# An attention block and two expert layers on one Trainium2 core: the second expert layer keeps its whole first expert unscaled, and three pieces of its order of work are rearranged

## The chip, the cores and the metric

The kernel runs on one core of a Trainium2 chip. The metric is the device time of one execution in microseconds (us), and of several executions the median. The kernel must return the reference's output, 3072 x 512 float32 numbers, to the accuracy asked for.

## What is computed

An attention over chunks, a first expert layer with one expert per token, and a second expert layer that runs all eight experts on every token. The change touches only the second layer. Cut to it, the reference is

```python
x = moe(attention(q, k, v, mem_k, mem_v))      # (N, D) = (3072, 512)
logits = x @ w_gate                            # (N, E), E = 8
P = np.exp(logits - logits.max())
for _ in range(8):                             # sinkhorn
    P /= P.sum(1, keepdims=True) + 1e-09
    P /= P.sum(0, keepdims=True) + 1e-09
    P *= N / E
out = np.zeros((N, D))
for e in range(E):
    h = np.maximum(x @ w1[e], 0.0)             # w1[e] is (512, 1024)
    out += P[:, e:e + 1] * (h @ w2[e])         # w2[e] is (1024, 512)
```

The plan P (a factor for each token and expert) needs eight rounds over all tokens before the first output can be scaled.

## The kernel before, in words

**Units.** Tokens are worked on in six blocks of 512 (NS = 6). An expert takes 12 units (EU), two for each block, one for each half of the hidden features; eight experts make 96 units, n = 0 to 95, and the loop over n runs to 96 so that the last outputs get done. Both products are done by a Strassen-like scheme of seven products (numbers 0 to 6) in place of eight, of 12 matmuls each, on operands that are split into a high and a low part, three matmuls for each piece of work. So a unit has 84 hidden matmuls (`h_mm`, L949 to L951), and among them stand the output matmuls of the unit before (`y_mm`, L1018 to L1020). The list TURN sets the order: "h0", "h1", "h5" and so on are hidden products, "y" is the next output product, "end" the end of the unit. Blocks end in units whose n is even ("even units"): there the last two output products (`y_tail`) come in as well, and the finished block is scaled and put out in the unit behind (an "odd unit").

**Hidden products.** `h_done` empties PSUM behind each product: for h0 ScalarE (ACT) copies the bank to the one that h1 adds to (L964), for the others ACT applies the relu (L916) or VectorE adds (L850). From the results, seven operands `cb0` to `cb6` for the output products are made: a cast to the high part on ACT (`c_hi`, L925 or L916) and a difference for the low part on VectorE (`c_lo`, L915 or L917). Those of cb5 and cb2 are in `h_rest`, at the unit's end.

**Outputs.** `y_done` and `y_end` gather a finished block in two tiles, oA and oB, one buffer each: ACT scales by P (`scaled`, L1035), VectorE adds with the factor (`plus`, L917). `keep_out` stores them: from GpSimd (POOL) as a DMA that adds to what stands in `out` (L1058), for the first expert otherwise. Its first three blocks end before P is ready; they are kept unscaled in `yd` (L1054), and the other three are scaled and stored plainly from SP (L1056). The three kept ones are fixed later, in units 11, 15 and 17 (the list FIX): `fix_load` reads them back into new oA and oB tiles behind h4 (L1092), and `fix_store` at the unit's end multiplies them on POOL (L1098) and stores them plainly from SP (L1099).

**Sinkhorn.** `sinks` hangs its steps behind products of units 1, 3, 5 and 7: the maximum (L1232, `sink_max1`), the exponential (`sink_exp`), then column steps (`sink_c`: one matmul into bank y3 of PSUM, a sum on VectorE) and row steps (`sink_a`).

**Weights.** Two raw tiles at a time are fetched and split for the next expert in units 11, 0 and 1 of an expert; QUOTA says how many pieces stand behind which product. `w2_parts` gives the four pieces of an output weight tile, a cast on ACT (L204) and a subtraction on VectorE (L208) each; `conv_subs` makes differences on POOL (L218) in tiles named `wtt` (two buffers). Units 1, 3, 5, 7 and 9 also prepare the next block of x (`prep_trans`, `prep_sums`, `prep_split`), in wtt, oA and oB.

**Queues.** Each engine runs its instructions in the order in which the program is written; SP issues all plain DMAs, POOL the adding ones.

## Time and profile before

| | |
|---|---|
| median of 3 runs | 2414.58 us (2413.73 to 2417.34) |
| the profiled execution's own time | 2411.26 us |
| its span | 2409.5 us |
| PE (TensorE) busy | 2314.5 us, 96% of the span |
| PEld (its weight loads) busy | 2264.0 us |
| VectorE (DVE) busy | 1512.9 us, 63% |
| ScalarE (ACT) busy | 1198.0 us, 50% |
| GpSimd (POOL) busy | 530.5 us, 22% |

The span is that of the traced instructions, on the clock by which all rows below are timed; the own time is what the same execution took on the device. PE and PEld work beside each other: a weight load runs while the matmul before it still does. A row of the view by stretch gives start and end, the length, the busy time (and the instructions) of PE, PEld, DVE, ACT and POOL, the granted clock, the DMA engines' share and GB/s. In rows of the trace tiles stand by their names with the buffer numbers left out. The granted clock (PEclk) is 1.00 for TensorE's full speed, the level of 2.4 GHz.

### The profile page before, as it was taken

To read this page: it belongs to the slowest core of one execution; us is meant where nothing else is said; L and a number is where in the kernel's file an instruction comes from. 1 tells how busy PE (TensorE), PEld (TensorE's weight loads), DVE (VectorE), ACT (ScalarE), POOL (GpSimd) and SP (SyncE) were. 2 spreads that over 40 slices of the span, in tenths; PEclk is the share of its full clock that TensorE was granted. 3 is DMA by queue.
4 is the path that set the end of the run, shared out by engine and by line. 5 is a ranking of instruction groups with operands and counts; after the bars stand their busy time and mean duration, and the time that the engine had idled before them with its cause. 6 is when DMAs were issued, how large, how long until landed. Compare 5 with 4: busy or idle time off the path is not lost.

```text
span 2409.5 us, 48142 instructions
## 1 busy us (share of the span) xinstructions
PE 2314.5 (96%) x19522; PEld 2264.0 (94%) x19522; DVE 1512.9 (63%) x2508; ACT 1198.0 (50%) x2482; POOL 530.5 (22%) x575
## 2 busy tenths in 40 slices
PE   8979996999989999999999999999999999999997
PEld 7869886899988999999999999999999999999997
DVE  5755666766765459555955595559554865586554
ACT  6744544444553346444644464446444554455443
POOL 3432234100332105000500050005100410141000
PEclk9989998999999999999999999999999999999999
DMA  9956643332544526453544355444534453545252
GB/s 232 261 154 196 201 151 136 126 146 110 205 150 133 174 80 181 126 142 96 166 142 126 112 149 158 111 127 141 166 101 136 140 167 91 146 132 149 82 155 36
DMA packets 154924, 345.35 MB, mean 143 GB/s; under 512 B 44552, under 2 KB 56968, under 8 KB 154698
## 3 DMA queue, kind: packets, MB, share of 16 engines
q1 hardware_dynamic: 128778, 291.45, 35.3%
q0 software_dynamic: 25920, 50.77, 12.5%
q8 instruction: 155, 2.54, 0.4%
q14 instruction: 71, 0.58, 0.1%
HBM read 257.76 MB, written 86.15 MB: 143 GB/s over the span
## 4 chain that ended last, share of the span: by engine, by line
PE 70%; DVE 10%; issue 8%; DMA 6%; ACT 3%; POOL 2%; SPq 0%; POOLq 0%; ACTq 0%; DVEq 0%
PE h_ps L949 11%; PE h_ps L950 11%; PE h_ps L951 10%; PE y_ps L1018 10%; PE y_ps L1019 10%; PE y_ps L1020 10%; DVE wl L208 4%; DMA qbd<-in_qT_dram 2%; DMA out_dram<-oB 2%; DVE r L915 1%; PE s_ps L271 1%; PE h_ps L739 1%; PE h_ps L740 1%; PE h_ps L738 1%; PE y_ps L756 1%
## 5 line engine op out<-in xcount | busy, mean ns | idle before, releaser
L949 PE MATMUL h_ps<-xs,wh 128*128 128x256 f32 x2688 | 766.7, 285 | 43.5 <-ACT r L916 18.7
L950 PE MATMUL h_ps<-xs,wh 128*128 128x256 f32 x2688 | 763.6, 284 | 0.0
L951 PE MATMUL h_ps<-xs,wl 128*128 128x256 f32 x2688 | 759.5, 283 | 0.0
L1018 PE MATMUL y_ps<-wh,cb 128*128 128x256 f32 x2304 | 652.2, 283 | 6.9 <-DVE r_s L902 4.6
L1019 PE MATMUL y_ps<-wl,cb 128*128 128x256 f32 x2304 | 649.6, 282 | 0.0
L1020 PE MATMUL y_ps<-wh,cb 128*128 128x256 f32 x2304 | 647.9, 281 | 0.0
L949 PEld LDWEIGHTS h_ps<-xs,wh 128*128 128x128 f32 x2688 | 509.5, 190 | 52.0 <-ACT r L916 20.8
L951 PEld LDWEIGHTS h_ps<-xs,wl 128*128 128x128 f32 x2688 | 512.3, 191 | 0.0
L950 PEld LDWEIGHTS h_ps<-xs,wh 128*128 128x128 f32 x2688 | 509.2, 189 | 0.1
L1018 PEld LDWEIGHTS y_ps<-wh,cb 128*128 128x128 f32 x2304 | 437.6, 190 | 8.8 <-DVE r_s L902 5.2
L915 DVE TENSOR_TENSOR cb<-r,cb 128x512 fp32r<-128x512 f32 x384 | 272.2, 719 | 269.5 <-ACT cb L925 269.5
L1020 PEld LDWEIGHTS y_ps<-wh,cb 128*128 128x128 f32 x2304 | 437.7, 190 | 0.0
L1019 PEld LDWEIGHTS y_ps<-wl,cb 128*128 128x128 f32 x2304 | 436.6, 189 | 0.0
L1058 POOL DMA_DIRECT2D out_dram<-oA x42 | 50.9, 1212 | 1312.4 <-ACT r L916 909.6
L925 ACT CAST cb<-r 128x512 fp32r<-128x512 f32 x384 | 239.3, 623 | 97.6 <-DVE r L917 70.7
L916 ACT ACTIVATE cb<-r 128x512 fp32r<-128x512 f32 x96 | 60.6, 632 | 289.1 <-DVE r L850 289.1
L916 ACT ACTIVATE r<-h_ps 128x512 f32<-128x512 f32 x191 | 114.1, 597 | 143.6 <-PE h_ps L951 142.4
L850 DVE TENSOR_TENSOR r<-h_ps,m 128x512 f32<-128x512 f32 x97 | 67.0, 691 | 187.0 <-PE h_ps L951 186.6
L208 DVE TENSOR_TENSOR wl<-wraw,wh 128x512 fp32r<-128x512 f32 (+2 forms) x150 | 146.7, 994 | 47.9 <-ACT wh L204 46.9
L218 POOL TENSOR_TENSOR wtt<-wraw 128x256 f32<-128x256 f32 x120 | 130.2, 1085 | 92.2 <-DVE wl L208 82.8
L964 ACT COPY h_ps<-h_ps 128x512 f32<-128x512 f32 x96 | 54.9, 572 | 176.8 <-PE h_ps L951 176.8
L915 DVE TENSOR_TENSOR r<-r,r 128x512 f32<-128x512 f32 x192 | 138.3, 720 | 3.3
(236 smaller groups left out, 3702.7 us busy)
## 6 DMA issues: line engine op xcount, KB each, us to landing
xs<-xd SPq DMA_DIRECT2D x294, 512.0 KB
wraw<-in_m_w_dram SPq DMA_DIRECT2D x124, 512.0 KB
xd<-xs SPq DMA_DIRECT2D x42, 512.0 KB
out_dram<-oA POOLq DMA_DIRECT2D x42, 512.0 KB, 6.4
out_dram<-oB POOLq DMA_DIRECT2D x42, 512.0 KB, 11.6
vw<-in_v_dram SPq DMA_DIRECT2D x40, 176.0 KB
qbd<-in_qT_dram SPq DMA_DIRECT2D x48, 128.0 KB
x_t<-x_nat SPq DMA_DIRECT2D x24, 256.0 KB
```

Of the source, the lines that this page charges most:

```text
L208: eng.tensor_tensor(out=lo, in0=src, in1=hi.bitcast(F32), op=ALU.subtract)
L218: sub = lambda o, a, b: nc.gpsimd.tensor_tensor(out=o, in0=a, in1=b, op=ALU.subtract)
L850: add = lambda o, a, b: nc.vector.tensor_tensor(out=o, in0=a, in1=b, op=ALU.add)
L915: tt = lambda o, a, b, op: nc.vector.tensor_tensor(out=o, in0=a, in1=b, op=op)
L916: relu = lambda o, i: nc.scalar.activation(out=o, in_=i, func=ACTF.Relu)
L925: (relu if pos else lambda o, i: nc.scalar.copy(out=o, in_=i))(cb[n, i][:, 0], src)
L949: nc.tensor.matmul(o, wh[:, i, k], x[:, 0, k], start=(new and f == 0 and k == 0), stop=False, skip_group_check=True)
L950: nc.tensor.matmul(o, wh[:, i, k], x[:, 1, k], start=False, stop=False, skip_group_check=True)
L951: nc.tensor.matmul(o, wl[:, i, k], x[:, 0, k], start=False, stop=(k == 1), skip_group_check=True)
L1018: nc.tensor.matmul(o, t[:, 0, c], wh, start=(i != 1 and half == f == j == 0), stop=False, skip_group_check=True)
L1019: nc.tensor.matmul(o, t[:, 0, c], wl, start=False, stop=False, skip_group_check=True)
L1020: nc.tensor.matmul(o, t[:, 1, c], wh, start=False, stop=(half == f == 1), skip_group_check=True)
```

## The change

Four things move, all in the second layer.

The whole first expert, six blocks, is kept unscaled in `yd`. Fixes come in units 16, 18, 20, 28, 30 and 32, one block each; they are read behind h0 into two `wtt` buffers, in place of oA and oB, are multiplied on POOL, and are added to `out` by a DMA from POOL. What first writes the rows of `out` is then the second expert, plainly, from POOL.

The sinkhorn's maximum and exponential go to unit 3 (behind h1 and h4), its column steps to h1 and h4 of units 5, 7, 9 and 11.

In the first unit, of the four pieces of each of the first two output weight tiles, pieces 0 and 3 go behind the add that ends the last product (`mid`), and pieces 1 and 2 into unit 1, behind h0. From there on `h_rest` of a unit stands behind h0 of the next one, and QUOTA has the pieces that stood behind h3 behind h2.

The last block reads the old rows of `out` back two units earlier (`last_load`) and adds them on chip, in an order of its own (`last_first`, `last_end`), so that two plain stores, from ACT and SP, end the program.

```diff
...
 NU2 = E * EU
+NUB = NU2 // 2
 XW = D + 2
...
     xd = [dram.tile([7, 128, 1024], F32, name=f"xd{s}") for s in range(NS)]
-    yd = [dram.tile([2, 128, 1024], F32, name=f"yd{s}") for s in range(3)]
+    yd = [dram.tile([2, 128, 1024], F32, name=f"yd{s}") for s in range(NS)]
     add = lambda o, a, b: nc.vector.tensor_tensor(out=o, in0=a, in1=b, op=ALU.add)
...
 
-    def h_done(n, i, late=False):
+    def h_done(n, i, late=False, mid=None):
         a, b = hb["a"], hb["b"]
...
             add(u2, a, u2)
+            if mid:
+                mid()
             tt(r21, r21, r11, ALU.subtract)
...
         o = O[b, h][:, :, d]
-        if b < 3:
+        if b < NS:
             if src is not None:
...
         o = O[b, h][:, :, d]
-        if b < 3:
+        if b < NS:
             add(o, src, o)
...
         o = O[b, h].rearrange("p j d f -> p j (d f)")
-        if b < 3:
+        if b < NS:
             nc.sync.dma_start(out=yd[s][h].rearrange("p (j d) -> p j d", j=2), in_=o)
-        elif b < NS:
-            nc.sync.dma_start(out=rows_of(s, h), in_=o)
+        elif b < 2 * NS:
+            nc.gpsimd.dma_start(out=rows_of(s, h), in_=o)
         else:
...
 
+    L = {}
+
+    def last_load(s):
+        for h in range(2):
+            t = raw.tile([128, 2, 512], F32, name="had", tag="wtt", bufs=2)
+            L[h] = t.rearrange("p j (d f) -> p j d f", d=2)
+            nc.sync.dma_start(out=t, in_=rows_of(s, h))
+
+    def last_scaled(h, d, src, on):
+        e, s = divmod(NUB - 1, NS)
+        for j in range(2):
+            stt(O[NUB - 1, h][:, j, d], src[:, j], P[:, 4 * s + 2 * h + j, e:e + 1], on[:, j, d], ALU.mult, ALU.add)
+
+    def last_first():
+        b = NUB - 1
+        m4 = halves(Y[b, 4])
+        o = O[b, 1]
+        scaled(b, 1, 1, None)
+        add(o[:, :, 0], o[:, :, 1], o[:, :, 0])
+        last_scaled(1, 1, m4, o)
+        add(o[:, :, 1], o[:, :, 1], L[1][:, :, 1])
+        nc.scalar.dma_start(out=rows_of(NS - 1, 1), in_=o.rearrange("p j d f -> p j (d f)"))
+        last_scaled(0, 1, O[b, 0][:, :, 1], L[0])
+        last_scaled(0, 1, m4, O[b, 0])
+
+    def last_end():
+        b = NUB - 1
+        last_scaled(0, 1, halves(Y[b, 2]), O[b, 0])
+        last_scaled(0, 0, halves(Y[b, 0]), L[0])
+        nc.sync.dma_start(out=rows_of(NS - 1, 0), in_=O[b, 0].rearrange("p j d f -> p j (d f)"))
+
     def y_done(b, i):
...
             O[b, 1] = o_tile(1)
-            scaled(b, 1, 0, halves(Y[b, 3]))
+            if b == NUB - 1:
+                last_scaled(1, 0, halves(Y[b, 3]), L[1])
+            else:
+                scaled(b, 1, 0, halves(Y[b, 3]))
         elif i == 0:
...
             add(O[b, 1][:, :, 1], halves(Y[b, 6]), O[b, 0][:, :, 1])
+            if b == NUB - 1:
+                last_first()
 
...
         for h in range(2):
-            fixes[s, h] = o_tile(h)
-            nc.sync.dma_start(out=fixes[s, h].rearrange("p j d f -> p j (d f)"), in_=yd[s][h].rearrange("p (j d) -> p j d", j=2))
+            fixes[s, h] = raw.tile([128, 2, 512], F32, name="fix", tag="wtt", bufs=2)
+            nc.sync.dma_start(out=fixes[s, h], in_=yd[s][h].rearrange("p (j d) -> p j d", j=2))
 
...
         for h in range(2):
-            t = fixes[s, h].rearrange("p j d f -> p j (d f)")
+            t = fixes[s, h]
             for j in range(2):
                 nc.gpsimd.tensor_scalar(out=t[:, j], in0=t[:, j], scalar1=P[:, 4 * s + 2 * h + j, 0:1], scalar2=None, op0=ALU.mult)
-            nc.sync.dma_start(out=rows_of(s, h), in_=t)
+            nc.gpsimd.dma_start(out=rows_of(s, h), in_=t, accum_op=ALU.add)
 
...
     hb["d"] = bank("h_ps", "y5")
-    todo = []
+    first = []
+
+    def first_mid():
+        for c in (0, 3):
+            for q in first:
+                q[c]()
+
     for k, i in enumerate(START):
...
         h_mm(0, i, True)
-        if k == 6:
-            for q in todo:
-                q.pop(0)()
-                q.pop(0)()
-        h_done(0, i, True)
+        h_done(0, i, True, first_mid if k == 6 else None)
         if k in (3, 4):
             first_subs(k - 3)
-            todo.append(w2_parts(E, k - 3))
-        if k == 5:
-            for q in todo:
-                q.pop(0)()
-                q.pop(0)()
-    h_rest(0)
+            first.append(w2_parts(E, k - 3))
     for i in range(7):
...
     x2_load(1)
-    assert not any(todo)
-    todo = []
+    todo = [q[c] for c in (1, 2) for q in first]
+    later = [lambda: h_rest(0)]
 
...
 
-    todo += [first_w2(2), first_w2(3)]
-    sinks = {(1, "h0"): lambda p: (nc.vector.tensor_reduce(out=m_p, in_=P, axis=AX.XY, op=ALU.max), sink_max1(p)), (1, "h1"): sink_exp}
-    steps = [(1, "h4")] + [(n, c) for n in (3, 5) for c in ("h1", "h4", "h6")] + [(7, "h1")]
+    start_w2 = [first_w2(2), first_w2(3)]
+    sinks = {(3, "h1"): lambda p: (nc.vector.tensor_reduce(out=m_p, in_=P, axis=AX.XY, op=ALU.max), sink_max1(p)), (3, "h4"): sink_exp}
+    steps = [(n, c) for n in (5, 7, 9, 11) for c in ("h1", "h4")]
     for c in steps:
...
 
-    QUOTA = {EU - 1: {"h0": 2, "h1": 2, "h6": 3, "h3": 1}, 0: {"h0": 4, "h1": 3, "h4": 1, "h6": 4, "h3": 2}, 1: {"h1": 2, "h4": 2, "h6": 4, "h3": 2}}
-    FIX = {EU - 1: 0, EU + 3: 1, EU + 5: 2}
-    later = []
+    QUOTA = {EU - 1: {"h0": 2, "h1": 2, "h6": 3, "h2": 1}, 0: {"h0": 4, "h1": 3, "h4": 1, "h6": 4, "h2": 2}, 1: {"h1": 2, "h4": 2, "h6": 4, "h2": 2}}
+    FIX = {EU + 4: 0, EU + 6: 1, EU + 8: 2, 2 * EU + 4: 3, 2 * EU + 6: 4, 2 * EU + 8: 5}
     for n in range(1, NU2 + 1):
...
         more = QUOTA.get(n if n < 1 else k, {})
+        if n == NU2 - 2:
+            last_load(NS - 1)
         if n == EU - 2:
...
         if n == 1:
-            more = {"h0": 2, "h1": 2, "h5": 2, "h4": 2, "h6": 2}
+            more = {"h1": 2, "h5": 2, "h4": 2, "h6": 2, "h2": 2}
         assert n != 2 or not todo
...
                 if not last:
-                    h_rest(n)
+                    if n == NU2 - 1:
+                        h_rest(n)
+                    else:
+                        later.append(lambda n=n: h_rest(n))
                     if prep:
...
                     y_tail(m // 2)
-                    later.append(lambda b=m // 2: y_end(b))
-                if last:
-                    later.pop()()
+                    if last:
+                        last_end()
+                    else:
+                        later.append(lambda b=m // 2: y_end(b))
                 if n in FIX:
...
                 h_done(n, i)
-                if later:
-                    later.pop()()
+                if n == 1 and i == 0:
+                    while todo:
+                        todo.pop(0)()
+                    todo += start_w2
+                while later:
+                    later.pop(0)()
                 if (n, c) in sinks:
                     sinks[n, c](bank("g_ps", "y3"))
-                if n in FIX and c == "h4":
+                if n in FIX and c == "h0":
                     fix_load(FIX[n])
```

Lines of the changed program lie one further down at first (L851 for L850, L916 for L915), and more behind `keep_out`. Three places show how the instructions move on their engines.

VectorE at the end of the first unit of the second layer, before. `u2<-h_ps` is the add that ends the last product; wl and vl are low parts of weights, `cb1` to `cb6` the low parts of hidden operands:

```order
L917 SCALAR_TENSOR_TENSOR r22_5550<-r22_5550,r21_5525 128x512
L208 TENSOR_TENSOR wl1_5505<-cb4_5499,wh1_5504 128x512
L208 TENSOR_TENSOR wl1_5505<-cb5_5385,wh1_5504 128x512
L208 TENSOR_TENSOR wl1_5534<-cb6_5528,wh1_5533 128x512
L208 TENSOR_TENSOR wl1_5534<-cb2_5387,wh1_5533 128x512
L208 TENSOR_TENSOR vl1_5507<-cb5_5385,vh1_5506 128x256
L208 TENSOR_TENSOR wl1_5505<-cb4_5499,wh1_5504 128x512
L208 TENSOR_TENSOR vl1_5536<-cb2_5387,vh1_5535 128x256
L208 TENSOR_TENSOR wl1_5534<-cb6_5528,wh1_5533 128x512
L850 TENSOR_TENSOR u2_5494<-h_ps_5537,u2_5494 128x512
L915 TENSOR_TENSOR r21_5525<-r21_5525,r11_5476 128x512
L915 TENSOR_TENSOR r11_5476<-r22_5550,r11_5476 128x512
```

And in the change:

```order
L851 TENSOR_TENSOR u2_5497<-h_ps_5540,u2_5497 128x512
L209 TENSOR_TENSOR wl1_5508<-cb4_5502,wh1_5507 128x512
L209 TENSOR_TENSOR wl1_5537<-cb6_5531,wh1_5536 128x512
L209 TENSOR_TENSOR wl1_5508<-cb4_5502,wh1_5507 128x512
L209 TENSOR_TENSOR wl1_5537<-cb6_5531,wh1_5536 128x512
L916 TENSOR_TENSOR r21_5528<-r21_5528,r11_5479 128x512
L916 TENSOR_TENSOR r11_5479<-r22_5553,r11_5479 128x512
L918 SCALAR_TENSOR_TENSOR m4_5526<-u2_5497,r11_5479 128x512
L916 TENSOR_TENSOR cb4_5583<-r22_5553,cb4_5583 128x512
L918 SCALAR_TENSOR_TENSOR cb1_5585<-u2_5497,cb1_5585 128x512
L916 TENSOR_TENSOR cb6_5587<-r21_5528,cb6_5587 128x512
L209 TENSOR_TENSOR wl1_5508<-cb5_5388,wh1_5507 128x512
```

The add stands ahead of all weight subtractions, of which four follow it and four more come behind `cb6`, in unit 1; the rest of cb5 and cb2 has moved behind them.

ScalarE at the end of unit 35 and the start of unit 36 (the first of the fourth expert), before. The copy of `h_ps` is that of h0; the lines L1035 scale a block that just ended:

```order
L925 CAST cb4_13952<-r22_13904 128x512
L916 ACTIVATE cb1_13954<-u2_13860 128x512
L925 CAST cb6_13956<-r21_13933 128x512
L925 CAST cb5_13987<-r11_13832 128x512
L925 CAST cb2_13989<-m4_13878 128x512
L964 COPY h_ps_5428<-h_ps_14022 128x512
L1035 ACTIVATE oA_13846<-y_ps_13621,P_5368 128x256 x2
L1035 ACTIVATE oA_13846<-oA_13846,P_5368 128x256 x2
```

And in the change:

```order
L926 CAST cb4_13958<-r22_13910 128x512
L917 ACTIVATE cb1_13960<-u2_13866 128x512
L926 CAST cb6_13962<-r21_13939 128x512
L965 COPY h_ps_5431<-h_ps_14022 128x512
L926 CAST cb5_14036<-r11_13838 128x512
L926 CAST cb2_14038<-m4_13884 128x512
L1038 ACTIVATE oA_13852<-y_ps_13627,P_5368 128x256 x2
L1038 ACTIVATE oA_13852<-oA_13852,P_5368 128x256 x2
```

The copy of h0 now stands ahead of the casts of cb5 and cb2, and these stand between it and the scaling of oA. The same holds at the start of every odd unit.

VectorE near the end of unit 36, where weights are split (`wl1<-wtt`) behind h3 before, and behind h2 in the change. First before:

```order
L917 SCALAR_TENSOR_TENSOR r22_14433<-r22_14433,r21_14481 128x512
L208 TENSOR_TENSOR wl1_14485<-wtt_14442,wh1_14484 128x512
L208 TENSOR_TENSOR wl1_14485<-wraw_14315,wh1_14484 128x512
L850 TENSOR_TENSOR u2_14385<-h_ps_14390,u2_14385 128x512
L915 TENSOR_TENSOR r21_14481<-r21_14481,r11_14344 128x512
L915 TENSOR_TENSOR r11_14344<-r22_14433,r11_14344 128x512
L917 SCALAR_TENSOR_TENSOR m4_14403<-u2_14385,r11_14344 128x512
L915 TENSOR_TENSOR cb4_14513<-r22_14433,cb4_14513 128x512
L917 SCALAR_TENSOR_TENSOR cb1_14515<-u2_14385,cb1_14515 128x512
L915 TENSOR_TENSOR cb6_14517<-r21_14481,cb6_14517 128x512
```

And in the change:

```order
L918 SCALAR_TENSOR_TENSOR r22_14439<-r22_14439,r21_14487 128x512
L851 TENSOR_TENSOR u2_14391<-h_ps_14396,u2_14391 128x512
L916 TENSOR_TENSOR r21_14487<-r21_14487,r11_14350 128x512
L916 TENSOR_TENSOR r11_14350<-r22_14439,r11_14350 128x512
L918 SCALAR_TENSOR_TENSOR m4_14409<-u2_14391,r11_14350 128x512
L916 TENSOR_TENSOR cb4_14506<-r22_14439,cb4_14506 128x512
L918 SCALAR_TENSOR_TENSOR cb1_14508<-u2_14391,cb1_14508 128x512
L916 TENSOR_TENSOR cb6_14510<-r21_14487,cb6_14510 128x512
L209 TENSOR_TENSOR wl1_14516<-wtt_14448,wh1_14515 128x512
L209 TENSOR_TENSOR wl1_14516<-wraw_14321,wh1_14515 128x512
```

Two subtractions (pieces of the weights for an output product of the next unit) have moved from ahead of the add to u2 to behind the rest of cb6.

## Rows read from the trace of the kernel before

**Rows 1.** One part of the profile's page, busy time of each engine, with the span.

```profile
span 2409.5 us, 48142 instructions
...
PE 2314.5 (96%) x19522; PEld 2264.0 (94%) x19522; DVE 1512.9 (63%) x2508; ACT 1198.0 (50%) x2482; POOL 530.5 (22%) x575
```

**Rows 2.** The view by stretch; units 1, 3, 9, 12, 16, 18, 28, 29, 36, 37.

```profile
402.32:434.44 32.12, 26.37 (x177) 25.48 (x178) 24.75 (x46) 15.43 (x30) 5.66 (x4) 0.81 0.14 56
455.89:481.46 25.57, 23.25 (x180) 22.72 (x179) 20.37 (x44) 9.18 (x17) 5.47 (x4) 0.93 0.26 104
594.07:615.15 21.08, 20.73 (x175) 20.35 (x173) 13.13 (x22) 10.20 (x21) 5.54 (x4) 1.00 0.25 95
656.32:686.50 30.18, 23.41 (x183) 23.20 (x182) 19.11 (x28) 15.01 (x30) 21.91 (x20) 0.89 0.46 163
745.16:774.82 29.66, 23.75 (x183) 23.55 (x182) 12.05 (x19) 8.98 (x17) 7.35 (x4) 0.88 0.32 122
793.42:822.37 28.95, 23.92 (x183) 23.71 (x181) 11.63 (x19) 8.98 (x17) 7.60 (x4) 0.88 0.31 116
1004.82:1026.27 21.45, 21.45 (x182) 21.45 (x181) 11.27 (x19) 9.32 (x17) 0.00 (x0) 1.00 0.09 36
1026.27:1044.87 18.60, 18.60 (x158) 18.60 (x157) 10.07 (x18) 8.71 (x17) 2.41 (x2) 1.00 0.78 209
1165.27:1188.21 22.94, 21.82 (x181) 21.62 (x181) 21.50 (x28) 15.17 (x30) 16.48 (x16) 1.00 0.42 144
1188.21:1208.17 19.96, 19.32 (x159) 18.76 (x158) 18.99 (x33) 13.58 (x29) 6.87 (x7) 1.00 0.68 175
```

**Rows 3.** PE's waits: engine and line, releaser, us in total, times, longest us.

```profile
PE h_ps L949 <- ACT r L916: 18.7, 5, 6.8
PE h_ps L949 <- DVE u L850: 9.9, 1, 9.9
PE h_ps L949 <- ACT h_ps L964: 8.3, 12, 1.1
```

**Rows 4.** ACT's waits, same columns.

```profile
ACT oB L1035 <- DMA out_dram<-oB: 19.9, 3, 9.6
```

**Rows 5.** Timeline of VectorE ahead of unit 1: start us, length us, what.

```profile
393.60 4.61 DVE L208 TENSOR_TENSOR wl<-cb,wh 128x512 fp32r<-128x512 f32 x4
...
401.58 0.68 DVE L850 TENSOR_TENSOR u<-h_ps,u 128x512 f32<-128x512 f32 x1
```

**Rows 6.** Timelines of ACT and the weight loads, weights' casts and unit 95.

```profile
959.44 1.14 ACT L204 CAST wh<-wtt 128x512 fp32r<-128x512 f32 x2
...
2367.38 0.57 ACT L964 COPY h_ps<-h_ps 128x512 f32<-128x512 f32 x1 [3.72 <-PE h_ps L951]
2367.86 0.85 ACT L1035 ACTIVATE oA<-y_ps,P 128x256 f32<-128x256 f32 x2
...
2369.87 0.19 PEld L1018 LDWEIGHTS y_ps<-wh,cb 128*128 128x128 f32 x1
```

**Rows 7.** The view by stretch: twelve matmuls behind a wait of 2.31 us, unit 3.

```profile
472.68:475.50 2.82, 2.82 (x13) 2.82 (x14) 2.61 (x8) 0.00 (x0) 0.81 (x1) 0.53 0.02 6
```

**Rows 8.** Timelines of VectorE and ACT at the end of the program.

```profile
2392.39 0.69 DVE L850 TENSOR_TENSOR oB<-y_ps,oA 128x512 f32<-128x512 f32 x1
...
2395.88 0.84 ACT L1035 ACTIVATE oA<-y_ps,P 128x256 f32<-128x256 f32 x2 [7.96 <-PE y_ps L1020]
...
2399.45 0.88 DVE L917 SCALAR_TENSOR_TENSOR oB<-y_ps,P,oB 128x256 f32<-128x256 f32 x2
```

**Rows 9.** Timeline of VectorE at an expert boundary, units 35 and 36.

```profile
1149.88 1.67 DVE L917 SCALAR_TENSOR_TENSOR oA<-y_ps,P,oA 128x256 f32<-128x256 f32 x4 [1.87 <-ACT oA L1035]
...
1184.80 1.23 DVE L208 TENSOR_TENSOR wl<-wtt,wh 128x512 fp32r<-128x512 f32 x1
```

**Rows 10.** The chain of waits around unit 17: start us, us, what.

```profile
786.88 6.70 DMA oA<-yd
...
801.41 2.80 DMA out_dram<-oB
```

## The prediction, on record before the changed kernel was run

> **What bounds the kernel now.** I read the page's span and busy lines first [rows 1], then what TensorE (PE) waited for, then its waits by unit, then the engine behind each wait. PE is busy 96% of 2409.5 us, so the change can only win time in which PE waits, runs at half clock, or has finished. A unit n of the second layer is 84 matmuls of hidden products for half a token block, with 72 or 96 output matmuls of unit n-1 between them. In the stretch view a plain even unit lasts 21.45 us and a plain odd one 18.60, with PE busy throughout [rows 2]; the reader is to measure every other unit against these two. The excesses lie in five places. Unit 1 lasts 32.12 us, and 9.9 us of wait stand ahead of it [rows 2, 3]; units 3 and 5 (alike) last 25.57 where an odd unit that also prepares a block of x lasts 21.08 (unit 9); units 12, 16 and 18 last 30.18 to 28.95; units 0 and 1 of each expert from the third on, 22.94 and 19.96 [rows 2]; and behind the last matmul, which ends at about 2396, 13.5 us of tail remain [rows 8]. What stands in the list of PE's waits names the releasers of the larger ones: `ACT r`, 18.7 us in 5, `DVE u`, 9.9 in one, `ACT h_ps`, 8.3 in 12 [rows 3].
>
> **Part 1, the fixes (units 12, 16, 18).** PE waits there for ACT, and ACT for the store of a fixed block: 19.9 us in 3 [rows 4]. `fix_load` takes the two output tiles oA and oB, so the next block's first write to oB waits until GpSimd has multiplied and the store has landed. The change gives the fixes the two `wtt` buffers, which lie idle in units 16 to 20 and 28 to 32, since weights are converted only in units 11, 0 and 1 of an expert. The three units last 30.18, 29.66 and 28.95 [rows 2] against 21.45 each: 24.4 us. Unit 12 and the one behind it then show the expert boundary that the others have (22.94 - 21.45 and 19.96 - 18.60, 2.9 us) and some of it returns from the sinkhorn part below: I take -20.5, bounds -24 and -17. Six fixes in place of three double GpSimd's multiplies and add 3 MB of stores and loads beside as many adding stores; they fall in units where GpSimd has nothing else to do, and nothing on PE's path reads what they write. I cost them at nothing. If that cover went, an adding store that lands late would be the first thing to show, and its buffers are wanted again some 20 us later at the earliest.
>
> **Part 2, the first unit.** PE's 9.9 us end with `DVE u`, the add that empties the bank that unit 1 writes. VectorE reaches it at 401.58, because eight weight subtractions stand ahead of it from 393.60 [rows 5]. In the new order the add stands ahead of them all, at 393.6, and PE starts unit 1 at about 394.3: 8 us earlier. What is late next: the four subtractions that follow the add (4.61 us, beside GpSimd) [rows 5] delay the two r differences, ACT's cast of one of them, and so ACT's copy of the first hidden product, which stands behind that cast. I get 401 for the copy, so PE waits some 2.5 us ahead of h1, then some 2 us ahead of its second output product for the other four subtractions. Of its 32.12 us PE is busy 26.37 now [rows 2]: the 5.75 of waits go with the sinkhorn's first steps and the eight subtractions, and these two come in their place. Half clock comes on top: behind a wait of 2.31 us twelve matmuls took 2.82 us at a granted 0.53 of the clock, which is half, the level of 1.2 GHz [rows 7]; at a plain unit's pace (18.60 us for 156) they take 1.4. I charge 1.3 us for each such wait. So unit 1 becomes 21.08 + 4.5 + 2.6 = 28.2 instead of 32.1, and the sum of the part is -8 - 4 = -12. Bounds: -8 (the later waits stay as large as now) and -15 (one of the two new ones vanishes, with its clock).
>
> The Trainium skill ("TensorE: Matmul & The Clock Gate", Part 1, on the clock gate) has the clock fall back to half only after a spell of idleness and return after sustained work, so that a short wait need not cost more than itself. By that, the half-speed matmuls I charge to two waits in unit 1 and to one and a half below would cost nothing, and the sum would be about 4.5 us better. The row of 0.53 behind 2.31 us speaks against it, and I go by the row.
>
> **Part 3, the sinkhorn.** Eight column steps move from units 1, 3, 5 and 7 to units 5, 7, 9 and 11, two each; the work is the same. What goes is the third step behind h6, whose bank y3 the very next output product wants: 2.31 us and half clock, twice (units 3 and 5), 3.6 us each [rows 7]. What comes: in unit 3 the maximum now stands on VectorE behind two casts' rests and the four adds of the block that ends, which the change also puts behind h0. I get 7.1 us into the unit for the maximum, where PE wants it at 4.5: 2.7 us and 1.3 of clock, so unit 3 stays near 25.5. Unit 5 falls by 3.4. Units 7 and 9 gain two steps and a wait of 0.5 us each for the copy that empties a transposing bank, about +1 each; unit 11, which prepares no block and so is shorter, makes the second step wait 1.4 us for the first, +2.8 with clock. Sum +1, bounds -4 and +4.
>
> **Part 4, h_rest behind the next h0, and two weight pieces behind h2.** On ACT two casts move from ahead of the copy of h0 to just behind it. At an expert boundary this ends the wait for `ACT h_ps` (1.1 us, mostly), since the copy no longer stands behind a cast that waits for VectorE. But VectorE bounds the boundary: it is busy 21.50 of 22.94 and 18.99 of 19.96 us [rows 2], and its work does not shrink. A pair of casts lasts 1.14 us, and ACT's next instruction begins 0.09 ahead of an end (the copy of 0.57 at 2367.38, the scaling at 2367.86) [rows 6]; so two casts ahead of the block's scaling make VectorE start that block's sums 1.05 us later; now it idles 1.87 us there [rows 9]. Some 0.6 comes back in a later idle stretch. And the two pieces that moved (1.23 us and as much [rows 9]) now stand behind the chain u, r, r, m and three rests; they hold the weights for the first output product of unit 1 of the expert, which PE wants about 2 us earlier than they are ready. The copy's waits go, this wait comes. For six boundaries +1 in all, bounds -8 (the copy's waits go and nothing comes) and +8 (both come).
>
> In the 41 plain odd units that scale a finished block (15 to 95) the two casts push ACT's scaling of oA, which empties the bank that the second output product starts. It starts at 2367.86 and takes 0.85 [rows 6]; 1.05 us later it ends at 2369.76. The weight load of that product starts at 2369.87 [rows 6]. With 0.05 us from an end to a start the margin is 0.06 us. I take +0.05 us for each, +2, with bounds 0 and +12 (0.3 each: a tenth of a microsecond late, and the weight load no longer hidden).
>
> **Part 5, the end.** Now: the last matmul ends at about 2396, ACT scales, VectorE ends at 2400.33 [rows 8], GpSimd issues the second adding store behind it, and the span ends 9.2 us behind VectorE. In the change the adds behind the sixth product end at 2393.08; then one scaling pair on ACT (0.85 [rows 6], with its start 0.9), an add (0.69), a pair from PSUM (0.88 [rows 8]), an add (0.69), and eight more pieces at 1.67 for four [rows 9]: 2399.6. The old rows of out come in two units earlier on an idle queue. The last store is a plain one from SP. The nearest rows are plain stores and loads of the same 512 KB from SP: 2.80 us, and 6.70 beside other traffic [rows 10]; at the end only the other half's store precedes it, so I take 3.5: 2403. That is -6, bounds -3 and -7.
>
> **Sum.** -20.5 - 12 + 1 + 1 + 2 - 6 = -34.5 us against the profiled execution's 2411.3, that is 2376.8. The median of the three runs shown, 2414.6, is 3.3 above it; the same step from there gives 2380.1.
>
> **Rivals.**
> The margin in the odd units fails by the whole shift: 41 waits of 1.05 us with the lost hiding of a weight load are some 45 us in place of 2, so 2423, slower. It decides where ACT's copy of h0 or either cast begins about 1 us later than now. For it: the margin is 0.06 us. Against it: their sources are ready some 4 us before, as ACT's idle stretch ahead of that copy shows (3.72 us [rows 6]). It fails by 0.2 us more easily: 0.3 each, 12 us, gives 2390.
> The boundaries and the first unit close better (-8 and -15): 2368. For it: PE's largest waits at the boundary name the copy. Against: VectorE is busy 94% of those two units.
> The change doesn't free the fixes, because ACT would wait for these tiles anyway, for the block before: -34.5 + 20.5, so 2401. Against: no other ACT wait for an `out_dram` store stands in the list than the three [rows 4].
>
> **How the numbers follow.** Forecast 0.60; better close 0.18; odd units late by a little 0.14; late by the whole shift 0.04; fixes not freed 0.04. Range 2363 to 2395: it holds the first three with the bounds of the end and the sinkhorn about them. A measurement of this kernel can tell 0.2%, 4.8 us. Every case but one lies further down than that: faster 0.95, same 0.01, slower 0.04.
>
> **What would show it.** Right: units 12, 16 and 18 near 23, 21.5 and 21.5; no ACT wait for `out_dram`; PE's wait ahead of unit 1 near 2 us; a new PE wait for a reduction of P in unit 3; a new PE wait for `DVE wl` at unit 1 of each expert; 7 to 8 us behind the last matmul. Wrong: plain odd units above 18.7, fixes that hold up GpSimd's stores, or an end bound by the load of the old rows.

## The result, and the profile after

The changed kernel takes 2383.85 us (median of 4 runs, 2382.68 to 2384.70) against 2414.15 for the kernel before in runs on the same chip: 30.3 us less, a ratio of 0.987 (95% interval 0.9855 to 0.9889). The forecast was 2380.1, in a range of 2363 to 2395. The profiled execution's own time is 2384.70. The page's span and busy lines after (before: [rows 1]):

```profile
span 2383.0 us, 48017 instructions
...
PE 2310.5 (97%) x19522; PEld 2262.7 (95%) x19522; DVE 1529.9 (64%) x2506; ACT 1166.7 (49%) x2458; POOL 548.0 (23%) x597
```

The view by stretch after, for units 0, 1, 2, 3, 9, 11, 12, 16, 18, 35, 36, 37, 41, 72 and 73 (the columns of [rows 2]):

```profile
381.49:396.27 14.78, 11.34 (x86) 10.73 (x84) 10.93 (x16) 8.88 (x16) 10.70 (x13) 0.95 0.86 281
396.27:427.15 30.88, 25.40 (x172) 24.51 (x173) 25.54 (x34) 15.10 (x30) 12.75 (x10) 0.83 0.35 131
427.15:450.42 23.27, 23.27 (x181) 23.06 (x181) 15.76 (x26) 11.35 (x21) 0.00 (x0) 0.93 0.41 150
450.42:475.93 25.51, 22.78 (x177) 22.25 (x176) 15.85 (x27) 9.86 (x19) 5.54 (x4) 0.93 0.20 79
586.17:607.81 21.64, 21.36 (x179) 20.89 (x177) 17.85 (x35) 9.51 (x18) 5.54 (x4) 1.00 0.23 93
630.14:650.82 20.68, 19.47 (x162) 19.30 (x161) 16.81 (x34) 11.08 (x21) 3.37 (x4) 1.00 0.66 238
650.82:673.36 22.54, 21.73 (x183) 21.53 (x182) 21.45 (x27) 14.16 (x28) 15.88 (x16) 1.00 0.33 109
733.01:754.47 21.46, 21.46 (x183) 21.46 (x181) 11.68 (x19) 8.32 (x15) 9.51 (x6) 1.00 0.53 114
773.07:794.52 21.45, 21.45 (x182) 21.45 (x181) 11.65 (x19) 8.31 (x15) 9.30 (x6) 1.00 0.53 117
1119.25:1138.57 19.32, 18.86 (x159) 18.66 (x157) 15.77 (x23) 10.94 (x24) 10.48 (x10) 1.00 0.75 200
1138.57:1164.16 25.59, 23.48 (x182) 23.07 (x181) 24.75 (x31) 16.27 (x32) 16.68 (x16) 0.93 0.39 138
1164.16:1182.76 18.60, 18.60 (x158) 18.60 (x157) 17.20 (x30) 12.81 (x27) 6.09 (x6) 1.00 0.75 191
1244.27:1262.87 18.60, 18.60 (x159) 18.60 (x157) 10.16 (x18) 9.20 (x18) 2.43 (x2) 1.00 0.74 194
1874.03:1898.14 24.11, 22.00 (x182) 21.59 (x181) 23.27 (x29) 16.18 (x32) 15.94 (x16) 1.00 0.42 146
1898.14:1917.99 19.85, 19.08 (x159) 18.73 (x157) 18.92 (x32) 12.76 (x26) 6.92 (x7) 1.00 0.67 176
```

Against [rows 2] the reader should see that units 16 and 18 are plain now, that unit 3 has stayed where it was, and that unit 36 has grown from 22.94 to 25.59 us with VectorE busy 24.75 of them.

The waits of PE and ACT after (the columns of [rows 3]):

```profile
PE h_ps L950 <- DVE r L851: 16.3, 14, 1.9
PE h_ps L950 <- DVE u L851: 4.5, 2, 2.6
PE y_ps L1022 <- DVE wl L209: 4.0, 5, 0.9
PE g_ps L885 <- DVE r_s L1268: 2.6, 1, 2.6
...
PE h_ps L950 <- ACT r L917: 2.2, 4, 0.6
PE h_ps L950 <- ACT h_ps L965: 1.7, 1, 1.7
```

```profile
ACT oB L1038 <- DMA out_dram<-oB: 1.1, 2, 0.9
```

Where the list of before named ACT [rows 3], it now names VectorE; the 19.9 us of [rows 4] are 1.1.

Where the time went, by the lengths of all units in the two traces:

| part | forecast | measured |
|---|---|---|
| fixes (units 12 to 18) | -20.5 | -22.4 |
| first unit and what follows (units 0 to 2) | -12 | -7.4 |
| sinkhorn (units 3 to 11) | +1 | 0.0 |
| expert boundaries (units 11, 0, 1, 2 of an expert, the six from units 23 to 26 on) | +1 | +7.0 |
| plain odd units | +2 | 0.0 |
| end, behind the last matmul | -6 | -5.7 |
| sum | -34.5 | -28.5 |

Ahead of unit 0, where nothing was changed, the profiled execution after is 1.9 us later (unit 0 began between 378.2 and 383.2 over the profiles of this study), so the spans differ by 26.6 (2409.51 less 2382.95). The first boundary (units 11 to 13) stands in the rows of the sinkhorn and the fixes.

### The profile page after: what moved, and what is told of

It reads as the page before. It is cut to its first block, busy times and chain, and to the rows that moved or that the text cites. A ratio compares the mean times of both kernels' runs of the same rounds, so it can differ in the third digit from the quotient of the medians.

```text
span 2383.0 us, 48017 instructions
## 1 busy us (share of the span) xinstructions
PE 2310.5 (97%) x19522; PEld 2262.7 (95%) x19522; DVE 1529.9 (64%) x2506; ACT 1166.7 (49%) x2458; POOL 548.0 (23%) x597
## 4 chain that ended last, share of the span: by engine, by line
PE 78%; DVE 11%; ACT 4%; issue 4%; DMA 2%; POOL 1%; SPq 0%; DVEq 0%; ACTq 0%; POOLq 0%
PE h_ps L950 12%; PE h_ps L951 12%; PE h_ps L952 11%; PE y_ps L1022 11%; PE y_ps L1021 11%; PE y_ps L1023 11%; DVE wl L209 5%; DVE cb L916 1%; ACT a L289 1%; PE h_ps L740 1%; PE h_ps L741 1%; PE h_ps L739 1%; PE y_ps L757 1%; PE y_ps L759 1%; PE y_ps L758 1%
## 5 line engine op out<-in xcount | busy, mean ns | idle before, releaser
L916 DVE TENSOR_TENSOR cb<-r,cb 128x512 fp32r<-128x512 f32 x384 | 276.8, 722 | 319.1 <-ACT cb L926 319.1
L1061 POOL DMA_DIRECT2D out_dram<-oA x35 | 42.2, 1207 | 1050.4 <-ACT r L917 772.4
L209 DVE TENSOR_TENSOR wl<-wraw,wh 128x512 fp32r<-128x512 f32 (+2 forms) x150 | 154.0, 1043 | 39.9 <-ACT wh L205 39.0
L851 DVE TENSOR_TENSOR r<-h_ps,m 128x512 f32<-128x512 f32 x97 | 66.8, 689 | 174.1 <-PE h_ps L952 173.7
L916 DVE TENSOR_TENSOR r<-r,r 128x512 f32<-128x512 f32 x192 | 135.7, 707 | 3.3
```

The source lines that it names most:

```text
L209: eng.tensor_tensor(out=lo, in0=src, in1=hi.bitcast(F32), op=ALU.subtract)
L851: add = lambda o, a, b: nc.vector.tensor_tensor(out=o, in0=a, in1=b, op=ALU.add)
L916: tt = lambda o, a, b, op: nc.vector.tensor_tensor(out=o, in0=a, in1=b, op=op)
```

## Experiments

All runs not called otherwise are the changed kernel with one edit. They ran on several chips, on which the kernel before took 2412.4 to 2414.2 us, so the times of two experiments compare to about 2 us; unit lengths are read from one profile each.

**The fixes alone**, in the kernel before (`FIX` and the second expert's plain stores moved with it):

```diff
-            fixes[s, h] = o_tile(h)
+            fixes[s, h] = raw.tile([128, 2, 512], F32, name="fix", tag="wtt", bufs=2)
...
-            nc.sync.dma_start(out=rows_of(s, h), in_=t)
+            nc.gpsimd.dma_start(out=rows_of(s, h), in_=t, accum_op=ALU.add)
...
-    FIX = {EU - 1: 0, EU + 3: 1, EU + 5: 2}
+    FIX = {EU + 4: 0, EU + 6: 1, EU + 8: 2}
```

> The kernel before with one part of the change alone: its three fixes are read into two wtt buffers in units 16, 18 and 20 behind the first product, multiplied, and added to out by GpSimd's DMA, and the second expert stores the rows of those three blocks plainly. The theory, that these units wait only because the fix holds the output tiles: units 12, 16 and 18 fall from 30.18, 29.66 and 28.95 us to about 23, 21.5 and 21.5, and the time by 22 us, to 2392. Rival (ACT would wait for these tiles anyway, for the block before): the waits stay with another store's name, and the time stays above 2408.

2390.13 us against 2413.23, ratio 0.9901 (0.9885 to 0.9918): -23.1. Units 12, 16 and 18 in the view by stretch:

```profile
659.30:680.83 21.53, 21.53 (x182) 21.49 (x181) 20.18 (x27) 13.91 (x28) 15.15 (x14) 1.00 0.38 125
741.00:762.45 21.45, 21.45 (x182) 21.45 (x181) 12.03 (x19) 9.30 (x17) 8.83 (x6) 1.00 0.52 116
781.06:802.51 21.45, 21.45 (x182) 21.45 (x181) 12.03 (x19) 9.30 (x17) 8.79 (x6) 1.00 0.51 114
```

So three quarters of the gain is this part, and three fixed blocks do as well as six. The edit moves the buffers, the units and the kind of store at once; that the buffers are what counted rests on [rows 4], where ACT waits for the store out of oB.

**The old end:**

```diff
-            if b == NUB - 1:
-                last_first()
...
-                        last_end()
+                        y_end(m // 2)
...
-        if n == NU2 - 2:
-            last_load(NS - 1)
```

> The changed kernel with the old end: no early load of the last block's old rows, ACT's three scalings and VectorE's sums behind the last matmul, and two adding stores from GpSimd. By the two traces 13.7 us stood behind the last matmul before and 8.0 in the changed kernel. Theory: the whole 5.6 us come back, 13.5 us behind the last matmul, and the time is 2389.5. Rival: part of what the old end lasted came from the traffic of the kernel before and not from its order; then less than 4 us come back.

2388.91 us (ratio to before 0.9897, 0.988 to 0.9913): 5.1 more than the changed kernel, with 14.3 us behind the last matmul. The theory holds.

**The first unit's old order** (one execution), all eight subtractions ahead of the add and `h_rest` of unit 0 at its end again:

```diff
...
-        h_done(0, i, True, first_mid if k == 6 else None)
+        if k == 6:
+            for q in todo:
+                q.pop(0)()
+                q.pop(0)()
+        h_done(0, i, True)
...
```

> The changed kernel with the first unit's old order: eight weight subtractions ahead of the add, h_rest of unit 0 at its end. The sinkhorn stays in its new units. Units 0 to 2 last 68.93 us in the changed kernel and 76.30 before. By the forecast's own sum the order is worth 8 us alone, the wait ahead of unit 1: then they last 76 to 77 us here. Theory from the two traces: VectorE bounds unit 1, so the earlier add only moves subtractions into it, and half of the 7.4 us came from the sinkhorn's first steps that left unit 1 (a wait of 2.40 us and the half clock behind it): then they last about 72 to 73 us.

2385.62 us. Units 0 to 2:

```profile
380.96:403.85 22.89, 11.47 (x85) 10.88 (x84) 18.88 (x24) 11.07 (x22) 16.98 (x18) 0.80 0.88 301
403.85:429.51 25.66, 23.73 (x172) 23.14 (x173) 19.07 (x28) 13.95 (x27) 5.86 (x4) 0.88 0.13 51
429.51:451.87 22.36, 21.79 (x181) 21.59 (x181) 14.82 (x24) 10.53 (x19) 0.00 (x0) 1.00 0.43 157
```

They last 70.9 us, against 76.3 before and 68.9 in the changed kernel. So 5.4 of the 7.4 us came with the sinkhorn's leaving unit 1 (and the casts of unit 1 moving into unit 2), and the order is worth 2.0 between these two profiles: the add stands 8 us earlier, but unit 1 then grows from 25.66 to 30.88, with VectorE's busy time from 19.07 to 25.54. Between profiles the changed kernel's order itself varies as much: over the eight runs that have it units 0 to 2 last 67.0 to 69.2 us, so the order is worth 2 to 4 us. VectorE in the changed kernel's unit 1:

```profile
396.13 4.09 DVE L209 TENSOR_TENSOR wl<-cb,wh 128x512 fp32r<-128x512 f32 x4
400.15 2.36 DVE L916 TENSOR_TENSOR r<-r,r 128x512 f32<-128x512 f32 x2
402.55 1.11 DVE L918 SCALAR_TENSOR_TENSOR m<-u,r 128x512 f32<-128x512 f32 x1
```

**Two more orders for unit 1** (one execution each): pieces 0 and 1 behind the add, with cb4 and cb6 behind unit 1's first copy; and the next pieces earlier.

```diff
-        for c in (0, 3):
+        for c in (0, 1):
...
-    todo = [q[c] for c in (1, 2) for q in first]
-    later = [lambda: h_rest(0)]
+    todo = [q[c] for c in (3, 2) for q in first]
...
+    later = [first_rest]
```

> The changed kernel with another order at the end of the first unit and in unit 1: behind the add pieces 0 and 1 of the weights instead of 0 and 3, then the r differences and cb1; pieces 3 and 2 and the operands cb4 and cb6 come behind the copy of unit 1's first product. In the changed kernel unit 1 waits 1.72 us for that copy, because it stands on ACT behind the cast of cb6, which waits for a difference on VectorE behind four subtractions; then 0.91 us for piece 1; and 32 matmuls run at half clock from 403.5 to 410.2. Theory: these two waits go and most of the half-clock stretch with them, so unit 1 lasts 25 to 28 us instead of 30.89. Rival: VectorE, busy 25.54 of 30.88 us in that unit, bounds it, and the waits come back behind other products; then unit 1 stays at 30 or more.

2380.79 us; unit 1 lasts 29.37, between the theory and the rival. The 1.72 and the 0.91 us went, but 2.21 came back behind ACT's relu, 1.5 behind the load of x, and 2.47 at the end, as the rival has it. What the unit lost is half clock (PE busy 22.90 us in place of 25.40), and with the order left alone unit 1 lasted 29.64 to 31.32 in eight profiles: a gain from this order is not shown.

```diff
-            more = {"h1": 2, "h5": 2, "h4": 2, "h6": 2, "h2": 2}
+            more = {"h1": 4, "h5": 2, "h4": 2, "h6": 2}
```

> The changed kernel with the next weight pieces of unit 1 taken two steps earlier (four behind product 1, none behind product 2). In the changed kernel VectorE idles 3.10 us at 409 and has two subtractions too many at the unit's end, where PE waits 2.64 us for its add, and unit 2 then starts at half clock and lasts 23.26 us instead of 21.45. Theory: two subtractions of 0.68 us fall into the idle stretch, the wait falls to about 1.3 us, and unit 2 gets back at least half of its 1.8 us: units 1 and 2 together 2 to 4.5 us shorter than the 54.15 of the changed kernel. Rival: the wait at the unit's end is set by GpSimd's sums of the next block, which make two subtractions of VectorE last 3.49 us, and stays above 2.3 us.

2379.97 us; units 1 and 2 last 52.68, 1.5 less, and the wait at the end of unit 1 fell from 2.64 to 1.02, so unit 2 lasts 22.33. In the eight profiles with the old order that wait is 2.6 and unit 2 lasts 23.3, so these 0.9 us are the edit's; the rest is within their spread. The mechanism holds, its size was taken too high. The copy's wait in unit 1 was 3.25 here, which the edit did not make: it is 3.2 in four of the eight profiles too, where the matmuls ahead of it ran at full clock. And of what both runs gain on the changed kernel, 1.5 us stand in unit 3: it waits 2.63 us as before, but at a granted 1.00 of the clock it lasts 24.00 in place of 25.51.

**The margin in the odd units:**

```diff
         c_hi(n, 5, ht[n, "r11"])
+        if n > 12 and n % EU in (2, 4, 6, 8):
+            nc.scalar.copy(out=cb[n, 5][:, 0], in_=ht[n, "r11"])
```

> The changed kernel with one cast to the high part of cb5 done twice (the same values again) in the 28 units with numbers 2, 4, 6 and 8 of experts 2 to 8, so that ACT scales the finished block 0.52 us later in the odd units behind them. In the changed kernel the scaling of oA ends at 1248.33 in unit 41, and the first weight load of the product that writes its bank starts at 1248.45: a margin of 0.12 us. Theory: that margin is real. Then each of the 28 odd units gets longer by 0.4 us (0.52 less the margin) or a little more, 11 us or more in all. Rival: the order of the two is accidental, the product doesn't wait for that scaling. Then these units stay at 18.60 us.

2399.47 us (one execution), 15.6 more. PE's waits, unit 41, and in it the scaling and the weight load that follows:

```profile
PE y_ps L1023 <- ACT oA L1040: 8.5, 28, 0.3
```

```profile
1248.43:1267.59 19.16, 18.85 (x159) 18.65 (x157) 10.16 (x18) 9.82 (x19) 2.43 (x2) 1.00 0.74 187
```

```profile
1252.30 0.83 ACT L1040 ACTIVATE oA<-y_ps,P 128x256 f32<-128x256 f32 x2
...
1253.19 0.19 PEld L1023 LDWEIGHTS y_ps<-wh,cb 128*128 128x128 f32 x1 [0.51 <-ACT oA L1040]
```

All 28 units wait, 0.31 us each, and last 0.56 longer: 28 x 0.56 = 15.7. Counted from the unit's start the scaling ends 0.64 us later than in the changed kernel (4.70 in place of 4.06; more than the 0.52 planned) and the weight load starts 0.58 later (4.76 in place of 4.18). So the margin is real and 0.06 us, half of the 0.12 between the two in the changed kernel: a load that waits for the scaling starts 0.06 behind its end. PE's wait is 0.31 of the 0.56; the other 0.25 stands in its busy time (18.60 to 18.85), which I take for the overlap of weight loads and matmuls that is lost there.

**The casts and the pieces apart.** First `h_rest` at the unit's end again, from unit 1 on:

```diff
-                    if n == NU2 - 1:
-                        h_rest(n)
-                    else:
-                        later.append(lambda n=n: h_rest(n))
+                    h_rest(n)
```

> The changed kernel with h_rest of every unit from unit 1 on put back at the unit's end; the weight pieces stay behind product 2. Theory A (the pieces are the cause of the new wait): unit 36 still waits near 1.9 us for VectorE ahead of product 3, and the wait of 1.1 us for the copy of the first product may come back on top, so unit 36 lasts 25.5 to 27 us and the time is 2384 to 2392. Rival B (the moved casts are the cause): unit 36 falls back to 22.9 and the time to about 2375. In the plain odd units both expect no change, 18.60 us.

2370.16 us, ratio to before 0.9823 (0.9806 to 0.9839): 13.7 us less than the changed kernel, 5 below rival B's number. By unit lengths, units 3 to 11 lose 6.2 us and the six boundaries 6.1. Units 3, 11, 35, 36 and 37:

```profile
448.52:470.00 21.48, 21.32 (x177) 20.76 (x176) 15.78 (x27) 8.82 (x17) 5.54 (x4) 1.00 0.24 94
623.47:642.70 19.23, 19.23 (x163) 19.23 (x162) 16.80 (x34) 10.33 (x20) 3.50 (x4) 1.00 0.71 256
1109.83:1128.43 18.60, 18.60 (x159) 18.60 (x157) 16.00 (x23) 10.50 (x22) 10.48 (x10) 1.00 0.81 211
1128.43:1152.16 23.73, 21.80 (x183) 21.48 (x181) 22.89 (x29) 16.14 (x33) 15.87 (x16) 1.00 0.40 146
1152.16:1172.19 20.03, 19.12 (x159) 18.71 (x157) 19.12 (x32) 12.48 (x26) 6.92 (x7) 1.00 0.69 173
```

Unit 3 loses its whole wait (25.51 to 21.48): VectorE reaches the maximum in time when the rests of cb5 and cb2 do not stand ahead of it. Unit 11 falls by 1.4, units 11 of the later experts by 0.7. But the wait of 1.9 us in unit 36 stays, as theory A said; the unit lasts 23.73 and not A's 25.5 or more, since no half clock follows the wait there (at two of the six boundaries it does, and unit 0 lasts 25.3). Then the pieces alone:

```diff
-    QUOTA = {EU - 1: {"h0": 2, "h1": 2, "h6": 3, "h2": 1}, 0: {"h0": 4, "h1": 3, "h4": 1, "h6": 4, "h2": 2}, 1: {"h1": 2, "h4": 2, "h6": 4, "h2": 2}}
+    QUOTA = {EU - 1: {"h0": 2, "h1": 2, "h6": 3, "h3": 1}, 0: {"h0": 4, "h1": 3, "h4": 1, "h6": 4, "h3": 2}, 1: {"h1": 2, "h4": 2, "h6": 4, "h3": 2}}
```

> The changed kernel with its two or one weight pieces put back behind product 3 instead of product 2 (all three places of QUOTA). In the changed kernel unit 0 of the fourth expert (unit 36) lasts 25.59 us against 22.94 before: PE waits 1.91 us there for VectorE's add ahead of product 3, and then runs some twenty matmuls at half clock. Theory A: the piece that moved behind product 2 is the cause. It frees a wtt buffer 5 us later in the unit, so GpSimd's differences move onto VectorE's weight subtractions, which then last 1.2 us instead of 0.68. Then unit 36 falls to 22 or below, because the old wait for the copy of the first product (1.1 us) stays away, and the five boundaries give back about 2.5 to 3.5 us each: 2370 in all. Rival B: the two casts that moved behind the copy are the cause. Then unit 36 stays near 25.6 and the time near 2384.

2381.09 us (ratio to before 0.9869, 0.9853 to 0.9886). Unit 36 falls to 22.80, but units 35 and 37 grow to 19.86 and 20.46, and new waits take the old one's place:

```profile
PE h_ps L950 <- DVE u L851: 12.5, 13, 2.6
PE y_ps L1021 <- ACT oA L1038: 7.2, 6, 1.2
```

The last is the scaling of oA, pushed by the two casts at the one odd unit that has more in front of it. So theory A named the cause of the wait in unit 36 and was wrong on the time: with the casts still moved, units 11, 0, 1 and 2 last 84.5 us (mean of the six boundaries), against 83.6 before and 84.8 in the changed kernel. With the casts back and the pieces moved they lasted 83.8. Then both of these edits:

> The changed kernel with both parts of its order undone: h_rest at the unit's end from unit 1 on, and the weight pieces behind product 3. Undoing the first alone gave 2370.2, undoing the second alone 2381.1, the changed kernel 2383.9. Theory C, from these two traces: in units 11, 0 and 1 of an expert both moves make VectorE late, and each alone leaves one wait (1.9 us ahead of product 3 of unit 0 with the pieces moved, 2.3 us about unit 1 with the casts moved). Then these three units are those of the kernel before, 18.85, 22.94 and 19.96 us in the experts from the fourth on: 61.7 in place of 62.4 with the casts alone put back, and the time is about 2366. Rival D: the pieces behind product 2 are a gain of their own once the casts are back, and the time rises above 2370.

2368.71 us (ratio 0.9818, 0.9801 to 0.9834); units 35 to 37 sum to 61.9 as before. Theory C holds in the units; the total is 2.7 above its number, and below rival D's. Then the casts and the piece of unit 11 only (the edit to `h_rest` above, and this):

```diff
-    QUOTA = {EU - 1: {"h0": 2, "h1": 2, "h6": 3, "h2": 1}, 0: {"h0": 4, "h1": 3, "h4": 1, "h6": 4, "h2": 2}, 1: {"h1": 2, "h4": 2, "h6": 4, "h2": 2}}
+    QUOTA = {EU - 1: {"h0": 2, "h1": 2, "h6": 3, "h3": 1}, 0: {"h0": 4, "h1": 3, "h4": 1, "h6": 4, "h2": 2}, 1: {"h1": 2, "h4": 2, "h6": 4, "h2": 2}}
```

> The changed kernel with h_rest at the unit's end and only the piece of unit 11 of an expert back behind product 3; units 0 and 1 keep theirs behind product 2. It tells which piece makes VectorE late ahead of product 3 of unit 0. Theory: the piece of unit 11 alone, because it frees the wtt buffer for GpSimd, whose differences otherwise run beside VectorE's subtractions in unit 0. Then the wait of 1.9 us in unit 0 goes and the units 11, 0 and 1 sum to 61.7 us or less. Rival: the two pieces of unit 0 are the cause by themselves (two subtractions earlier in VectorE's queue), and the wait of 1.9 us stays, 62.4 us for the three.

2365.83 us (ratio 0.9807, 0.9791 to 0.9824). Units 35 to 37:

```profile
1107.33:1126.17 18.84, 18.77 (x159) 18.56 (x157) 16.24 (x24) 10.67 (x23) 11.06 (x11) 1.00 0.83 214
1126.17:1149.11 22.94, 21.82 (x180) 21.62 (x181) 21.43 (x28) 16.29 (x32) 16.48 (x16) 1.00 0.43 146
1149.11:1169.10 19.99, 19.18 (x159) 18.77 (x158) 19.06 (x32) 12.44 (x26) 6.85 (x7) 1.00 0.70 179
```

The wait in unit 36 is gone: the piece of unit 11 alone made it. The pieces of units 0 and 1 are a small gain where they are, which is rival D in part: units 11, 0, 1 and 2 last 83.1 here, 83.5 with all pieces back. Last, on top of that, the casts moved at that one place only:

```diff
-                    h_rest(n)
+                    if n % EU < EU - 1 or n == NU2 - 1:
+                        h_rest(n)
+                    else:
+                        later.append(lambda n=n: h_rest(n))
```

> The best kernel so far (h_rest at the unit's end, the piece of unit 11 behind product 3; 2365.8), but with h_rest of unit 11 of each expert, and of it alone, behind the next unit's first product. There PE still waits 1.2 us for the copy of that product, which stands on ACT behind a cast that waits for VectorE. Theory: at this one place the move does what it was made for, since unit 0 scales no block: the copy's wait goes, unit 0 falls from 22.94 to about 21.9 us in each of six experts, and the time by 3 to 6 us. Rival: VectorE is the bound in that unit (busy 21.5 us of it), its late rest comes up as another wait, and units 11, 0 and 1 together stay within 0.3 us of 61.7.

2369.56 us (ratio 0.9816, 0.98 to 0.9833), 3.7 more. Unit 36 falls to 21.56 and unit 37 rises to 21.57, where PE now waits for weights:

```profile
PE y_ps L1022 <- DVE wl L209: 16.7, 8, 2.4
```

The rival holds in kind, VectorE bounds these units and a wait removed on ACT comes back behind it, but not in size: the three units last 61.6 to 62.0 at three of the six boundaries and 63.1 to 63.2 at the others.

**A version of the parts that paid** (the pieces and casts of the run at 2365.83, with both changes to unit 1, of which the first is in part another):

```diff
-    todo = [q[c] for c in (1, 2) for q in first]
+    todo = [q[2] for q in first]
...
+                if (n, c) == (1, "h1"):
+                    first_rest()
```

> The best kernel so far (2365.8), with unit 1 changed as well: the next weight pieces two steps earlier, as in the run that made units 1 and 2 together 1.5 us shorter, and the first unit's order with pieces 0 and 1 behind the add; pieces 2 and h_rest then follow the copy of the first product, and pieces 3 with cb4 and cb6 come behind product 1, so that ACT's relu of that product does not stand behind casts that wait for VectorE (2.21 us in the other order tried). Theory: what remained in units 1 and 2 are waits on the order of ACT and VectorE, so units 0 to 2 together fall from 68.9 to 63 to 66 us, and the time to about 2361. Rival: VectorE's work in unit 1 bounds the three units whatever its order, and they stay above 67 us.

2365.44 us (ratio 0.9807, 0.9789 to 0.9825); units 0 to 2 last 67.4, above 67 as the rival has it. That VectorE's work alone bounds them stays open: in unit 1 PE waits 4.2 us for a copy on VectorE, but 2.3 us for the load of x too. The run stands level with the one at 2365.83, and both beat the changed kernel by 18 us, or 16 by their ratios to the kernel before.

## Why the prediction held, and where it missed

The sign, the order of size and the range were right. The sum came closer than its terms: two were too optimistic by 11 us together, and three too pessimistic by 5, which was luck. By its steps:

- **Part 1** was right, mechanism and size: units 12, 16 and 18 last 22.54, 21.46 and 21.45, and the part alone gave -23.1. Doubling GpSimd's multiplies cost nothing that shows on PE (units 16 and 18 are plain); two waits of ACT for a store (1.1 us) were left where I had expected none.
- **Part 2** was too large by 4.6 us, a little outside its bounds (over the eight profiles with this order the gain is 7.1 to 9.3). The 8 us ahead of unit 1 came (its wait is 1.84 now). What failed is "So unit 1 becomes 21.08 + 4.5 + 2.6 = 28.2": it lasts 30.88. The two waits that the sum names came smaller, 1.72 and 0.91 where 2.5 and 2 stood; a third of 2.64 at the unit's end was not in it; and the half clock took some 4.7 us, not 2.6 (PE is busy 25.40 us, against 20.73 in unit 9 before [rows 2]), most of it in the stretch behind the copy:

```profile
403.50:410.27 6.77, 5.86 (x28) 5.56 (x28) 5.13 (x10) 2.49 (x6) 0.00 (x0) 0.51 0.04 14
```

  Unit 2 pays 1.8 more in half clock, behind the third wait. I took subtractions out of PE's way without asking whether VectorE had room for them in unit 1. It is busy 25.54 of 30.88 us, and of the other orders of unit 1 one moved the waits about and one took the third away, for 0.9 us that are clear of the spread.
- **Part 3** was right: the wait for the maximum is 2.64 (2.7 forecast), unit 3 lasts 25.51 (25.5), unit 5 fell by 3.9 (3.4), unit 11 rose by 2.1 (2.8). Units 7 and 9 rose by 0.2 and 0.6 (1 each), and of the even units between, which the sum left out, 4 and 6 rose by 0.8 each. What the sum held as the price of the sinkhorn's new place is the price of the moved casts, which it named for unit 3 alone: with these put back, unit 3 falls by 4.0 us and units 3 to 11 by 6.2, so the sinkhorn's move by itself is worth -6 in these units and not +1.
- **Part 4** was mis-sized at the boundaries: +1 forecast, +7.0 measured. I priced the late weights in unit 1 of an expert (they came: 0.8 us in four experts), but not the add ahead of product 3 in unit 0, where PE waits 1.9 us for VectorE. The cause of that wait is the piece that went behind product 2 in unit 11, by the run that put it back. As I read the trace, it frees GpSimd's buffer later, GpSimd's differences fall beside VectorE's subtractions in unit 0, and these last 1.2 us in place of 0.68 (a 128x512 subtraction of these kinds with no GpSimd arithmetic beside it lasts 0.69 at most in this layer):

```profile
1149.83 1.22 DVE L209 TENSOR_TENSOR wl<-wtt,wh 128x512 fp32r<-128x512 f32 x1
1150.98 1.22 DVE L916 TENSOR_TENSOR cb<-r,cb 128x512 fp32r<-128x512 f32 x1
1152.12 1.21 DVE L209 TENSOR_TENSOR wl<-wtt,wh 128x512 fp32r<-128x512 f32 x1
1153.25 0.68 DVE L851 TENSOR_TENSOR r<-h_ps,m 128x512 f32<-128x512 f32 x1
```

```profile
1150.46 1.19 POOL L219 TENSOR_TENSOR wtt<-wraw 128x256 f32<-128x256 f32 x1
1151.61 1.17 POOL L219 TENSOR_TENSOR wtt<-wraw,wtt 128x256 f32<-128x256 f32 x1
```

  But the pieces are the smaller part of the 7.0 us: putting the casts back alone took 6.1 of them away, putting the pieces back alone 2.0. The term that was mis-sized is mostly the casts': the copy's waits went, as forecast, but what the later casts make late costs more.
- The plain odd units stayed at 18.60 (0.05 more each was forecast); they are 28, since 12 of the 41 counted lie at the boundaries and unit 95 ends the program. oA's scaling ends at 1248.33 in unit 41 and the weight load starts at 1248.45. The margin of 0.06 us is what the run on the margin found, so the rival of the whole shift was that near.
- **Part 5** was right: 8.0 us behind the last matmul, of which VectorE takes 3.7 as forecast, and the last store and what follows it 4.3 (3.5).
- **The half clock** was charged at 1.3 us a wait, and that was too regular. Units 36 and 72 have the same waits (2.11 us in all); in 36 the granted clock was 0.93 and the unit lasts 25.59, in 72 it was 1.00 and 24.11. By the rule as the prediction draws it from the Trainium skill ("TensorE: Matmul & The Clock Gate", Part 1) the waits here would have cost only themselves; unit 72 agrees and unit 36 does not.

## What to carry to other kernels

Before an instruction is moved off one engine's path, look at the busy time of the engine that must take it in that stretch: where it is near the stretch's length, as VectorE's 21.5 of 22.94 us, the wait only changes its name. A reorder made for one place (the copy at an expert's start) should be tried apart, since its price may fall elsewhere: here it cost 13.7 us that the gain of the other parts hid, half of it far from the expert's start, and at that one place alone it still lost 3.7. A piece that frees another engine's buffer also sets when that engine runs, and so what it runs beside.

## What the runs showed of the hardware that was not expected

The same wait does not always cost the clock. A wait of 1.84 us ahead of unit 1 was followed by half clock (the level of 1.2 GHz) in the changed kernel, and a wait of 1.85 at the same place, behind the same matmuls, by full clock in the run with pieces 0 and 1. The program need not differ: in the run with the casts back and in the one with casts and pieces back, whose programs are the same up to there, the wait is 1.87 both times, and the granted clock behind it 0.54 and 1.00. The view by stretch behind the wait, first in the changed kernel, then in the run with pieces 0 and 1:

```profile
396.27:400.02 3.75, 3.75 (x18) 3.75 (x19) 3.75 (x4) 0.90 (x2) 3.67 (x4) 0.54 1.01 397
```

```profile
395.33:396.87 1.54, 1.54 (x13) 1.54 (x13) 1.54 (x2) 0.61 (x1) 1.54 (x2) 1.00 0.97 378
```

And half clock may be nearly free: unit 36, slowed, and unit 37 sum to 44.19 us, units 72 and 73, not slowed, to 43.96. Unit 37 has no wait left, while PE waits 0.8 us for weights from VectorE in unit 73; I take it that VectorE catches up while PE runs slowly.
